# Attention, gated MLP and routed MLP on one Trainium2 core: the attention's value matmuls per head and per half of the array's columns, with two batches side by side

## The chip, the cores and the metric

The kernel runs on one NeuronCore of a Trainium2 chip. The metric is the device time of one execution in microseconds (us), lower is better. The core has TensorE (PE in the profile; PEld is its weight loading), VectorE (DVE), ScalarE (ACT), GpSimd (POOL) and SyncE (SP, which only issues DMAs here). Before the change three runs took 828.89, 834.08 and 834.34 us; the median is 834.08.

## What is computed

Three stages follow each other. Causal attention with a window of 64 keys, 4 batches, 8 heads, 576 tokens, head size 64:

```python
scores = scale * np.matmul(q, k.transpose(0, 1, 3, 2))
mask = (rel >= 0) & (rel < window)
scores = np.where(mask, scores, -1000000000.0)
scores = scores - np.max(scores, axis=-1, keepdims=True)
attn = np.exp(scores)
attn = attn / (np.sum(attn, axis=-1, keepdims=True) + 1e-09)
out = np.matmul(attn, v)
```

Its output becomes x, 2304 tokens by 512. A gated MLP follows (RMS norm, two 512 by 1536 matrices, silu(g) * val, a 1536 by 512 matrix), then a mixture of 8 experts in which each token goes to the one expert with the largest logit (512 to 1024, relu, 1024 to 512, times the gate). All of it is fp32; the MLPs split each operand into two fp32r parts and use three matmuls for one.

## The kernel before, in words

The order of instructions on every engine is written out by hand; nothing is moved by a scheduler. The attention works on units u = 0 to 15, one unit for a batch and a pair of heads (`b, hp = divmod(u, NHP)`), and on groups g = 0 to 47, three groups for a unit, three blocks of 64 queries for a group. The main loop `for g in range(NG + LX)` runs one step for each group and, in the same step, later stages of earlier groups. In step g these are:

- `scores(g)`, TensorE: one bf16 matmul puts the mask into bank g % 3 (384 columns), three fp32 matmuls add the scores of a block each. The stationary operand is `q_t`, 64 queries of head 0 beside 64 queries of head 1 with zeros off the diagonal, so that a block is 128 rows (two heads by 64 queries) by a window of 128 keys.
- `maxima(g)` on VectorE and `softmax(g - 1)` (three Exp) on ScalarE.
- `transposes(g - 3)` on TensorE into bank 3 or 4, and `pt_copy(g - 3)`, which copies 128 by 384 to SBUF, on ScalarE.
- `pv(g - 4)`, line 242, on TensorE: three fp32 matmuls of 128 by 130 columns, 128 values of both heads and two columns of ones for the sum. Only the two diagonal quarters of the result are used. The banks are 5, 6 and 7 in turn.
- `xo_out(g - 5)`, line 250, on VectorE: add 1e-9 to the sums, reciprocal, multiply into an SBUF tile; after a unit's third group two DMAs write it to `xdram` in DRAM, 64 floats at a time.

`q_place(u)` (line 193) fills `qz`, three buffers in turn, from the loaded q, for u from 2 on with two GpSimd instructions of 64 partitions each. It stands two units ahead of the scores that read it. `q_load`, `k_load` and `v_load` issue the loads on SP's queue, in the order of the program.

Beside the steps, `attending_work(g)` (line 524) advances generators a piece at a time: the RMS norms of the first two stretches of 384 tokens (`norm`, line 327, from steps 20 and 31 on, `G_NORM`), which read x back from `xdram`, the splitting of the first weights, and the unpacking of MLP weights on VectorE and ScalarE (`w_conv`), under a budget of `CREDIT` for each step. In the last five steps (48 to 52) the MLP's first matmuls (`first_gv`) are mixed in. After the loop the MLP goes over the 2304 tokens in blocks; `norm(2)` to `norm(5)` run beside it. All matmuls go through one helper on line 60.

Of the kernel before, what the change touches and what calls it, by code (L numbers as in the profile page):

```python
# [8 lines left out]
F32 = mybir.dt.float32  # L9
# [4 lines left out]
ALU = mybir.AluOpType  # L14
# [27 lines left out]

LT, LV, LX = 3, 4, 5
NQK = 3
VW = P + 2
G_MORE = 27, 42
G_LOAD, G_LAND, G_NORM = (3, 8, 13), 5, (15 + LX, 26 + LX)
CREDIT = 0.45
MID = 2.0
BUDGET = [4.6, 3.4, 4.7, 5.4]  # L50
# [3 lines left out]
def attention_moe_moe_kernel(ctx, tc, qT, kT, vw, w1p, rms_g, wg2, wg2T, w2p, out):  # L54
# [44 lines left out]
        nc.gpsimd.iota(tot, pattern=[[NT // P, E]], base=0, channel_multiplier=0,  # L99
                       allow_small_or_imprecise_dtypes=True)  # L100

    xdram = [dram.tile([S, DM], F32, name=f"xdram{b}") for b in range(B)]
    x2dram = dram.tile([NT + 1, DM], F32, name="x2dram")

    xs = dram.tile([E * NT, DM], F32, name="xs")
# [42 lines left out]
    def place(k, key, what):  # L148
# [3 lines left out]
        if not here:  # L152
# [11 lines left out]
    qz = [f_p.tile([P, NBLK, P], F32, name=f"qz{i}") for i in range(NQK)]  # L164
    vbuf = [t[:, a:a + 8 * VW].rearrange("p (w c) -> p w c", c=VW)
            for t, a in ((wraw_t[3], 0), (wraw_t[3], 8 * VW), (wraw_t[1], 5 * 3 * P))]

    def zeros(i):
        for h in range(2):
# [8 lines left out]
    NG = NU * 3  # L178
    q_t, qs_t, k_t, v_t, xo_t, p_t, pt_t, nm_t = {}, {}, {}, {}, {}, {}, {}, {}

    def q_load(u):
        if u < NU:
            qs_t[u] = a_q.tile([P, 64, NBLK], F32, name="qs")
            nc.sync.dma_start(qs_t[u], qT[u // NHP, u % NHP])

    def k_load(u):
        if u < NU:
            k_t[u] = a_q.tile([P, S], F32, name="kt")
            cuts = [0, 192, S] if u == 0 else [0, S]
            for c in (slice(*x) for x in zip(cuts, cuts[1:])):  # L190
                nc.sync.dma_start(k_t[u][:, c], kT[u // NHP, u % NHP, :, c])

    def q_place(u):
        if u < NU:
# [10 lines left out]
    def v_load(u):  # L205
        if u < NU:
            v_t[u] = vbuf[u % 3]
            nc.sync.dma_start(v_t[u][:, :, :P], vw[u // NHP, u % NHP])

    def scores(g):  # L210
        u, i0 = g // 3, 3 * (g % 3)
# [25 lines left out]

    def pt_copy(g):
        pt = pt_t[g] = wraw_t[1][:, (g % 5) * 3 * P:(g % 5 + 1) * 3 * P]
        nc.scalar.copy(pt, bank[3 + g % 2][:, 0:3 * P])  # L240

    def pv(g):
        u, i0 = g // 3, 3 * (g % 3)
        pt = pt_t.pop(g)
        for j in range(3):
            i = i0 + j
            w = 0 if i <= 1 else (i // 2 if i % 2 else 3 + i // 2)
            mm(bank[5 + g % 3][:, j * VW:(j + 1) * VW], pt[:, j * P:(j + 1) * P], v_t[u][:, w], True, True)

    def xo_out(g):  # L250
        u, i0 = g // 3, 3 * (g % 3)
        b, hp = divmod(u, NHP)
        if g % 3 == 0:
            t, a = ((wraw_t[4], 3 * DM), (wraw_t[5], 3 * DM), (wraw_t[2], 5 * 3 * P))[u % 3]
            xo_t[u] = t[:, a:a + 2 * S].rearrange("p (i c) -> p i c", c=P)
        vb = bank[5 + g % 3][:, 0:3 * VW].rearrange("p (j c) -> p j c", j=3)
        rs = a_s.tile([P, 3], F32, name="rs")
        nc.vector.tensor_scalar(out=rs, in0=vb[:, :, P], scalar1=1e-9, scalar2=None, op0=ALU.add)
        nc.vector.reciprocal(rs, rs)
        nc.vector.tensor_tensor(out=xo_t[u][:, i0:i0 + 3], in0=vb[:, :, :P], in1=rs.unsqueeze(2).to_broadcast([P, 3, P]),  # L260
                                op=ALU.mult)
        if g % 3 == 2:
            for h in range(2):
                r = slice(64 * h, 64 * h + 64)
                nc.sync.dma_start(xdram[b].rearrange("(i q) (a d) -> a q i d", q=64, d=64)[2 * hp + h], xo_t[u][r, :, r])

    class Task:

# [58 lines left out]
    def norm(i):  # L327
        t0, nt, _ = subs[i]
        T = nt // P
        if i == 1:  # L330

            xr, sq = (t[:, :3 * DM].rearrange("p (j d) -> p j d", d=DM) for t in wraw_t[:-3:-1])
        else:
            if i > 2:
                yield "step"
            xr, sq = big(0), big(1)
        for j in range(T):
            p = 0
            while p < P:
                b, s = divmod(t0 + j * P + p, S)  # L340
                step = min(P - p, S - s)
                nc.sync.dma_start(xr[p:p + step, j], xdram[b][s:s + step])
                p += step
        for _ in range(4 if i < 2 else 1):
            yield "wait" if i < 2 else "step"
        ss, y, t = (n_p.tile([P, 3], F32, name=x)[:, :T] for x in ("ss", "y", "nt"))
        for j in range(T):
            yield "act" if i < 2 else "rest"
            nc.scalar.activation(sq[:, j], xr[:, j], AF.Square, scale=1.0, accum_out=ss[:, j:j + 1])
        yield "wait" if i < 2 else "step"  # L350
        nc.vector.tensor_scalar(out=ss, in0=ss, scalar1=1.0 / DM, scalar2=1e-6, op0=ALU.mult, op1=ALU.add)
        nc.vector.tensor_scalar(out=y.bitcast(I32), in0=ss.bitcast(I32), scalar1=-0.5, scalar2=1597463007.0,
                                op0=ALU.mult, op1=ALU.add)
        sc = 1.0
        for _ in range(NEWTON):

            yield 0.35
            nc.vector.scalar_tensor_tensor(out=t, in0=y, scalar=1.0 / (sc * sc), in1=y, op0=ALU.mult, op1=ALU.mult)
            nc.vector.tensor_mul(t, t, ss)
            nc.vector.scalar_tensor_tensor(out=y, in0=t, scalar=-3.0, in1=y, op0=ALU.add, op1=ALU.mult)  # L360
            sc = sc * -2.0
        yield "wait" if i < 2 else 0.5
        for j in range(T):
            (nc.gpsimd if i < 2 else nc.vector).tensor_scalar(
                out=xr[:, j], in0=xr[:, j], scalar1=y[:, j:j + 1], scalar2=None, op0=ALU.mult)
            yield "wait" if i < 2 else 0.6
        staged[0] = True
        for _ in (4, 2, 0)[min(i, 2)] * [0]:
            yield "wait"
        if i >= NXT:  # L370
            yield lambda: free[0] >= i - NXT + 1
        xh_t[i], xl_t[i] = xh, xl = xt_views(i % NXT * 8 * SUB, nt)
        for c in range(4):
            bk = yield "bank"
            for j in range(T):
                nc.tensor.transpose(bk[:, j * P:(j + 1) * P], xr[:, j, c * P:(c + 1) * P], ident)
            nc.scalar.activation(xh[:, c], bk[:, :nt], AF.Copy, scale=gs_sb[:, c:c + 1])
            if i < 2:
                yield "wait"
            nc.vector.scalar_tensor_tensor(out=xl[:, c], in0=bk[:, :nt], scalar=gs_sb[:, c:c + 1],  # L380
                                           in1=xh[:, c].bitcast(F32), op0=ALU.mult, op1=ALU.subtract)
            if c < 3 and i > 1:
                yield 0.6
        normed[0] = i
        yield 0.6
# [138 lines left out]
    def attending_work(g):  # L524
        if not w64:
            ready.update(range(4))
        for i in st_t:
            loaded.setdefault(i, g)
        landed.update(i for i in st_t if g >= loaded[i] + G_LAND)
        tasks = [norm0] * (g >= G_NORM[0]) + [norm1] * (g >= G_NORM[1]) + [early] * (g >= G_LOAD[0])  # L530
        late[0] = g >= NG - 10
        for _ in range(2 if ending[0] else 1):
            busy = False
            for t in tasks + [acts] * w64:
                if not t.done and (t.want in (None, "wait") or t.want == "act" and not busy):
                    if t.want == "act":
                        busy = True
                    t.piece()
        c = min(credit[0] + (1.0 if ending[0] else CREDIT), 1.0 if ending[0] else 0.6)
        tasks = [t for t in tasks + [conv] if not t.done and t.want not in ("wait", "act")]  # L540
        if any(t.want == "bank" for t in tasks):
            on_bank(tasks, bank[5 + (g - 2) % 3])
            c -= 0.6
        if g >= G_LOAD[0] and converted[0] < 2:
            c = beside(tasks, c)
        elif g >= G_LOAD[0]:
            c = beside(tasks[:-1], c)
        credit[0] = c
# [31 lines left out]
    for g in range(NG + LX):  # L580
        if g == NG:
            ending[0] = True
            convert(1, conv)
            early.finish()
            norm0.finish(bank[2])
        if g < NG:
            if g % 3 == 0:
                q_load(g // 3 + 3)
# [3 lines left out]
            scores(g)  # L592
        if 0 <= g - LT < NG:
            transposes(g - LT)
        if 0 <= g - LV < NG:
            pv(g - LV)
        if g >= NG:
            for _ in range(2):
                next(first_gv, None)
        if 0 <= g - LT < NG:  # L600
            pt_copy(g - LT)
        if 0 <= g - LX < NG:
            xo_out(g - LX)
        if g < NG:
            maxima(g)
        if 0 < g <= NG:
            softmax(g - 1)
        if 0 < g < NG and g % 3 == 0:
# [6 lines left out]
        if g == 0:  # L615
            zeros(2)
            for v in vbuf:
                nc.vector.memset(v[:, :, P:], 1.0)
            q_place(2)
            constants()  # L620
        if g == 1:
# [657 lines left out]
```

## Time and profile before

| | us |
|---|---|
| three runs, median | 834.08 (828.89 to 834.34) |
| the profiled execution, its own time | 828.35 |
| its span, first to last instruction | 826.6 |
| attention, first score matmul to the first matmul of the MLP's second layer | 4.3 to 111.2 |

The profiled execution is 5.73 us below the median and close to the fastest run. The profile counts a matmul as busy until its result is out, so the starts of successive matmuls, not their durations, tell what one costs; every fp32 matmul stands as two matmul records (and two weight loads), so three matmuls of the program are six in a row. "x6" behind a row is the number of instructions merged in it. The idle time at a row's end is that of the engine just before, with what ended it.

### The profile page before, as it was taken

Reading aid. Unit: us, or ns where it says so; the run is one execution under the profiler, and the core shown is the slowest. Engines: PE = TensorE matmul, PEld = TensorE weight load, DVE = VectorE, ACT = ScalarE, POOL = GpSimd, SP = SyncE. Lnnn points to the kernel's source line nnn. Section 1 sums busy time; section 2 is a strip of 40 time slices with the busy share of each in tenths; the row PEclk is TensorE's granted clock in tenths of the full one; section 3 lists DMA queues with packets and bytes.
Section 4 is the critical chain, followed back from the end, with each engine's and each line's share of the span. In section 5 each row is a group of like instructions: output and inputs, shape, how many; then the busy total and the mean of one; then the engine's idle time right before and its main releaser. Section 6 shows DMA issues by size and latency. Waiting matters only on the chain. (4 is left out here: it accounts for less than half of the span.)

```text
span 826.6 us, 13258 instructions
## 1 busy us (share of the span) xinstructions
PE 806.6 (98%) x4777; PEld 746.5 (90%) x4777; DVE 566.7 (69%) x1210; ACT 431.1 (52%) x839; POOL 222.1 (27%) x194
## 2 busy tenths in 40 slices
PE   7999999999999999999999999999899999999997
PEld 7999989899999999999899999999788999888886
DVE  6898777777754766763389869846595765776454
ACT  5878877677633323322343333434564654765353
POOL 7989444334340000015000006031300220222021
PEclk9999999999999999999999999999999999999999
DMA  8999679889422101002110023861675763772010
GB/s 273 327 294 303 154 183 249 224 174 273 128 103 77 38 1 39 1 1 76 40 38 1 1 81 112 266 170 62 159 252 193 232 231 113 260 252 81 2 45 22
DMA packets 76179, 114.33 MB, mean 138 GB/s; under 512 B 28847, under 2 KB 45615, under 8 KB 75954
## 3 DMA queue, kind: packets, MB, share of 16 engines
q1 hardware_dynamic: 71506, 103.50, 42.5%
q0 software_dynamic: 4576, 9.47, 3.1%
q8 instruction: 69, 1.13, 0.6%
q14 instruction: 28, 0.23, 0.1%
HBM read 93.90 MB, written 31.10 MB: 151 GB/s over the span
## 5 line engine op out<-in xcount | busy, mean ns | idle before, releaser
L60 PE MATMUL bank<-xt,wha 128*128 128x384 f32 (+3 forms) x1728 | 417.9, 327 | 1.9 <-ACT xt L892 1.3
L60 PEld LDWEIGHTS bank<-xt,wha 128*128 128x128 f32 x1728 | 301.8, 188 | 10.9 <-ACT xt L892 1.5
L60 PE MATMUL bank<-xt,wla 128*128 128x384 f32 (+3 forms) x864 | 280.0, 324 | 0.3 <-DVE wla L576 0.3
L60 PEld LDWEIGHTS bank<-xt,wla 128*128 128x128 f32 x864 | 162.7, 188 | 1.0 <-DVE wla L576 0.6
L60 PE MATMUL bank<-who,hl 128*128 128x512 f32 x382 | 150.2, 393 | 1.0 <-DVE hl L1058 0.6
L60 PE MATMUL bank<-who,hh 128*128 128x512 f32 x382 | 150.3, 393 | 0.2 <-ACT x L1086 0.2
L60 PE MATMUL bank<-wlo,hh 128*128 128x512 f32 x382 | 149.4, 391 | 0.0
L685 ACT CAST hh<-t 128x384 fp32r<-128x384 f32 x72 | 37.0, 514 | 149.4 <-DVE t L684 149.4
L576 DVE TENSOR_TENSOR wla<-wraw,wha 128x512 fp32r<-128x512 f32 (+1 forms) x113 | 99.2, 878 | 15.9 <-ACT wha L574 15.2
L1058 DVE SCALAR_TENSOR_TENSOR hl<-bank,hh 128x512 fp32r<-128x512 f32 (+1 forms) x71 | 44.7, 629 | 70.9 <-ACT hh L1057 70.8
L684 DVE TENSOR_TENSOR t<-t,bank 128x384 f32<-128x384 f32 x72 | 39.7, 552 | 74.1 <-PE bank L60 67.9
L574 ACT CAST wha<-wraw 128x512 fp32r<-128x512 f32 (+1 forms) x113 | 87.0, 770 | 6.0 <-DVE wraw L426 5.8
L1087 POOL DMA_INDIRECT out_dram<-x,ix x32 | 34.8, 1086 | 204.1 <-ACT x L1086 196.6
L60 PEld LDWEIGHTS bank<-who,hl 128*128 128x128 f32 x382 | 71.8, 188 | 18.2 <-DVE hl L1058 1.4
L1057 ACT ACTIVATE hh<-bank 128x512 fp32r<-128x512 f32 (+1 forms) x71 | 39.0, 550 | 89.3 <-PE bank L60 89.3
L60 PEld LDWEIGHTS bank<-who,hh 128*128 128x128 f32 x382 | 72.0, 189 | 10.4 <-ACT x L1086 0.4
L60 PEld LDWEIGHTS bank<-wlo,hh 128*128 128x128 f32 x382 | 72.0, 189 | 10.2
L574 ACT CAST who<-wraw 128x512 fp32r<-128x512 f32 x111 | 68.7, 619 | 17.5 <-PE bank L60 17.5
L749 DVE SCALAR_TENSOR_TENSOR junk<-x,wg_bc 128x512 f32<-128x512 f32 x120 | 76.6, 685 | 0.0
L576 DVE TENSOR_TENSOR wlo<-wraw,who 128x512 fp32r<-128x512 f32 x99 | 68.2, 689 | 8.6 <-ACT who L574 3.4
L683 ACT ACTIVATE t<-bank 128x384 f32<-128x384 f32 x72 | 35.0, 486 | 65.7 <-PE bank L60 62.7
L797 POOL TENSOR_TENSOR tot<-tot,ohb 128x8 f32<-128x8 f32 x18 | 4.5, 251 | 237.6 <-DVE de L781 236.5
(154 smaller groups left out, 969.9 us busy)
## 6 DMA issues: line engine op xcount, KB each, us to landing
wraw<-in_w2p_dram SPq DMA_DIRECT2D x64, 512.0 KB, 4.6
st<-in_w1p_dram SPq DMA_DIRECT2D x24, 768.0 KB, 7.3
wraw<-in_vw_dram SPq DMA_DIRECT2D x16, 512.0 KB, 5.9
xs<-x2dram SPq DMA_DIRECT2D x8, 1024.0 KB, 12.8
qs<-in_qT_dram SPq DMA_DIRECT2D x16, 288.0 KB, 5.9
xdram<-wraw SPq DMA_DIRECT2D x32, 144.0 KB, 4.6
x2dram<-x SPq DMA_DIRECT2D x18, 256.0 KB, 2.0
kt<-in_kT_dram SPq DMA_DIRECT2D x15, 288.0 KB, 5.4
```

Of the source, the lines that this page charges most:

```text
L60: nc.tensor.matmul(o, l, r, start=start, stop=stop)
L574: nc.scalar.copy(wh, src[:, r])
L576: e.tensor_tensor(out=wl, in0=src[:, r], in1=wh.bitcast(F32), op=ALU.subtract)))
L683: nc.scalar.activation(t, g, AF.Silu, scale=1.0)
L684: nc.vector.tensor_tensor(out=t, in0=t, in1=v, op=ALU.mult)
L685: nc.scalar.copy(hh[:, :nt], t)
L749: nc.vector.scalar_tensor_tensor(out=junk, in0=x2, scalar=1.0, in1=wg_bc[:, e], op0=ALU.mult, op1=ALU.mult, accum_out=lg[:, j, e:e + 1])
L797: nc.gpsimd.tensor_tensor(out=tot, in0=tot, in1=ohb[:, j], op=ALU.add)
L1057: nc.scalar.activation(hh[:, :n], bank[k % 2][:, :n], AF.Relu, scale=1.0)
L1058: nc.vector.scalar_tensor_tensor(out=hl[:, :n], in0=bank[k % 2][:, :n], scalar=0.0, in1=hh[:, :n].bitcast(F32), op0=ALU.max, op1=ALU.subtract)
L1087: d = nc.gpsimd.indirect_dma_start(out=out[:, :], in_=y, in_offset=None, out_offset=bass.IndirectOffsetOnAxis(ap=ix[:, j, 0:1], axis=0), b ...
```

## The change

`of(u)` lets units of two batches alternate: units 0, 2, 4, 6 are batch 0 and 1, 3, 5, 7 batch 1, for the four pairs of heads; units 8 to 15 are batches 2 and 3. Two successive units make a super-unit of 18 blocks, of which two successive blocks are 128 tokens. `pv(d)` now takes six blocks, once in two steps. For each pair of blocks, head and block of the pair it issues one matmul with 64 stationary columns (the head's 64 queries) and 66 moving columns (the head's 64 values and two ones); the block decides whether the result goes to partitions 0 to 63 or 64 to 127. Twelve such matmuls fill one bank (6 or 7) as 128 tokens by two heads, three times. `xo_out(d)` divides this once in two steps. For the first two batches it writes straight into `x_sb`, three SBUF tiles in places of `wraw` that are free then, which `norm(0)` to `norm(2)` read without a DMA. For the other two it writes to `xdram`, 128 floats at a time. `pt_copy` of even groups moves from ScalarE to VectorE, behind `maxima`. Bank 5 is now free for the norms' transposes. The norms start at steps 25 and 33, and two weight loads move (`G_MORE`).

```diff
-VW = P + 2
-G_MORE = 27, 42
-G_LOAD, G_LAND, G_NORM = (3, 8, 13), 5, (15 + LX, 26 + LX)
+VW = P + 4
+G_MORE = 21, 44
+G_LOAD, G_LAND, G_NORM = (3, 8, 13), 5, (20 + LX, 28 + LX)
...
+    x_sb = [wraw_t[t][:, a:a + 3 * DM].rearrange("p (j d) -> p j d", d=DM) for t, a in ((4, 0), (4, 3 * DM), (5, 0))]
...
+    def of(u):
+        return 2 * (u // (2 * NHP)) + u % 2, u % (2 * NHP) // 2
...
     def pt_copy(g):
         pt = pt_t[g] = wraw_t[1][:, (g % 5) * 3 * P:(g % 5 + 1) * 3 * P]
-        nc.scalar.copy(pt, bank[3 + g % 2][:, 0:3 * P])
-
-    def pv(g):
-        u, i0 = g // 3, 3 * (g % 3)
-        pt = pt_t.pop(g)
+        (nc.scalar.copy if g % 2 else nc.vector.tensor_copy)(pt, bank[3 + g % 2][:, 0:3 * P])
+
+    def pv(d):
+        su, n0 = d // 3, 6 * (d % 3)
         for j in range(3):
-            i = i0 + j
-            w = 0 if i <= 1 else (i // 2 if i % 2 else 3 + i // 2)
-            mm(bank[5 + g % 3][:, j * VW:(j + 1) * VW], pt[:, j * P:(j + 1) * P], v_t[u][:, w], True, True)
+            for h in range(2):
+                for c in range(2):
+                    n = n0 + 2 * j + c
+                    u, i, at = 2 * su + n // NBLK, n % NBLK, n % 3 * P + 64 * h
+                    w = 0 if i <= 1 else (i // 2 if i % 2 else 3 + i // 2)
+                    mm(bank[6 + d % 2][64 * c:64 * c + 64, j * VW + 66 * h:j * VW + 66 * h + 66],
+                       pt_t[6 * su + n // 3][:, at:at + 64], v_t[u][:, w, 66 * h:66 * h + 66], True, True)
...
-        nc.vector.tensor_scalar(out=rs, in0=vb[:, :, P], scalar1=1e-9, scalar2=None, op0=ALU.add)
+        nc.vector.tensor_scalar(out=rs, in0=vb[:, :, 0:VW:VW - 2], scalar1=1e-9, scalar2=None, op0=ALU.add)
         nc.vector.reciprocal(rs, rs)
-        nc.vector.tensor_tensor(out=xo_t[u][:, i0:i0 + 3], in0=vb[:, :, :P], in1=rs.unsqueeze(2).to_broadcast([P, 3, P]),
-                                op=ALU.mult)
-        if g % 3 == 2:
-            for h in range(2):
-                r = slice(64 * h, 64 * h + 64)
-                nc.sync.dma_start(xdram[b].rearrange("(i q) (a d) -> a q i d", q=64, d=64)[2 * hp + h], xo_t[u][r, :, r])
+        nc.vector.tensor_tensor(out=xo.rearrange("p j (h d) -> p j h d", h=2),
+                                in0=vb[:, :, 2:P + 2].rearrange("p j (h d) -> p j h d", h=2),
+                                in1=rs.unsqueeze(3).to_broadcast([P, 3, 2, 64]), op=ALU.mult)
+        if bp:
+            rows = slice(part * 3 * P, (part + 1) * 3 * P)
+            nc.sync.dma_start(xdram[rows, cols].rearrange("(j p) c -> p j c", p=P), xo)
...
-            on_bank(tasks, bank[5 + (g - 2) % 3])
+            on_bank(tasks, bank[6 + (g - 3) // 2 % 2] if g % 2 else bank[5])
...
-        if 0 <= g - LV < NG:
-            pv(g - LV)
+        if 0 <= g - LV < NG and (g - LV) % 2:
+            pv((g - LV) // 2)
```

On TensorE, two steps in the middle of the attention, before. The rows are line, operation, output bank, moving and stationary operand; bank 65 to 67 hold scores, 68 and 69 transposes, 70 to 72 values:

```order
L60 LDWEIGHTS ident_b
L60 MATMUL bank_67<-maskb,ident_b 128x384
L60 MATMUL bank_67<-kt,qz_159 128x128 x3
L236 MATMUL bank_69<-ident,wraw_123 128x128 x3
L60 MATMUL bank_71<-wraw_122 128x130 x3
L60 LDWEIGHTS ident_b
L60 MATMUL bank_65<-maskb,ident_b 128x384
L60 MATMUL bank_65<-kt,qz_160 128x128 x3
L236 MATMUL bank_68<-ident,wraw_123 128x128 x3
L60 MATMUL bank_72<-wraw_122 128x130 x3
```

The same place now:

```order
L60 LDWEIGHTS ident_b
L60 MATMUL bank_67<-maskb,ident_b 128x384
L60 MATMUL bank_67<-kt,qz_156 128x128 x3
L240 MATMUL bank_69<-ident,wraw_120 128x128 x3
L60 LDWEIGHTS ident_b
L60 MATMUL bank_65<-maskb,ident_b 128x384
L60 MATMUL bank_65<-kt,qz_157 128x128 x3
L240 MATMUL bank_68<-ident,wraw_120 128x128 x3
L60 MATMUL bank_71<-wraw_119 64x66 x12
```

The three value matmuls of each step became twelve in every second step, each a quarter of the size, with the full array in use right before and right behind them.

On VectorE, two steps of the same stretch, before (the sums, reciprocal, product and maxima of a step):

```order
L258 TENSOR_SCALAR rs<-bank_71 128x3
L259 RECIPROCAL rs<-rs 128x3
L260 TENSOR_TENSOR wraw_125<-bank_71,rs 128x384
L224 TENSOR_REDUCE nm<-bank_65 128x3
L258 TENSOR_SCALAR rs<-bank_72 128x3
L259 RECIPROCAL rs<-rs 128x3
L260 TENSOR_TENSOR wraw_125<-bank_72,rs 128x384
L224 TENSOR_REDUCE nm<-bank_66 128x3
```

Two steps now:

```order
L268 TENSOR_SCALAR rs<-bank_72 128x6
L269 RECIPROCAL rs<-rs 128x6
L270 TENSOR_TENSOR wraw_123<-bank_72,rs 128x3x128
L228 TENSOR_REDUCE nm<-bank_66 128x3
L228 TENSOR_REDUCE nm<-bank_67 128x3
L244 COPY wraw_119<-bank_68 128x384
```

One division for two steps instead of two, and a copy that ScalarE did.

## Rows read from the trace of the kernel before

**Rows 1.** The page: span, TensorE's busy time, granted clock in 40 slices.
```profile
span 826.6 us, 13258 instructions
PE 806.6 (98%) x4777; PEld 746.5 (90%) x4777; DVE 566.7 (69%) x1210; ACT 431.1 (52%) x839; POOL 222.1 (27%) x194
...
PEclk9999999999999999999999999999999999999999
```

**Rows 2.** Busy by window: PE, PEld, DVE, ACT, POOL; clock, DMA share, GB/s.
```profile
12.50:93.00 80.50, 79.12 (x687) 77.47 (x685) 70.55 (x202) 65.92 (x197) 71.30 (x41) 1.00 1.04 305
93.00:108.00 15.00, 12.69 (x93) 11.75 (x91) 9.59 (x27) 9.30 (x23) 2.62 (x3) 1.00 0.25 44
```

**Rows 3.** Timeline of PE: one step at 59 us, and the start of step 45.
```profile
59.05 0.33 PE L60 MATMUL bank<-maskb,ident_b 128*128 128x384 bf16 x1
59.21 0.83 PE L60 MATMUL bank<-kt,qz 128*128 128x128 f32 x6
59.88 0.49 PE L236 MATMUL bank<-ident,wraw 128*128 128x128 f32 x3
60.20 0.83 PE L60 MATMUL bank<-wraw 128*128 128x130 f32 x6
60.88 0.33 PE L60 MATMUL bank<-maskb,ident_b 128*128 128x384 bf16 x1
...
89.33 0.33 PE L60 MATMUL bank<-maskb,ident_b 128*128 128x384 bf16 x1
```

**Rows 4.** Groups by form, 0 to 110 us: count, busy, mean ns, idle before.
```profile
L60 PE MATMUL bank<-wraw,wraw 128*128 128x130 f32 x198 | 27.6, 276 | 0.1
...
L260 DVE TENSOR_TENSOR wraw<-bank,rs 128x384 f32<-128x384 f32 x48 | 26.8, 558 | 1.6
L224 DVE TENSOR_REDUCE nm<-bank 128x3 f32<-128x384 f32 x48 | 26.4, 550 | 2.6 <-PE bank L60 1.4 <-PE bank L236 0.4 <-issue 0.3
L259 DVE RECIPROCAL rs<-rs 128x3 f32<-128x3 f32 x48 | 8.4, 176 | 1.7
L258 DVE TENSOR_SCALAR rs<-bank 128x3 f32<-128x3 f32 x48 | 7.4, 154 | 4.8 <-PE bank L60 4.7
...
L240 ACT COPY wraw<-bank 128x384 f32<-128x384 f32 x48 | 25.1, 523 | 12.9 <-PE bank L236 12.7
...
L202 POOL TENSOR_SCALAR qz<-qs 64x576 f32<-64x576 f32 x29 | 65.1, 2244 | 9.4 <-DMA qs<-in_qT_dram 6.6 <-PE bank L236 0.7 <-PE bank L376 0.4
```

**Rows 5.** Timeline of PE: small bf16 and fp32 matmuls of the routing.
```profile
368.25 0.27 PE L60 MATMUL bank<-ohb,ones_b 128*128 128x40 bf16 x5
368.37 0.18 PE L60 MATMUL bank<-totb,ones_b 128*128 128x48 bf16 x1
...
539.72 0.18 PE L60 MATMUL bank<-short,ones_b 1*128 1x24 bf16 x1
539.83 0.19 PE L60 MATMUL bank<-totb,ones_b 128*128 128x24 bf16 x1
...
566.22 2.74 PE L60 MATMUL bank<-wg_sb,x 128*128 128x8 f32 x24
568.81 0.37 PE L60 MATMUL bank<-xt,wha 128*128 128x256 f32 x1
```

**Rows 6.** Timeline of POOL in the attention.
```profile
16.12 32.91 POOL L202 TENSOR_SCALAR qz<-qs 64x576 f32<-64x576 f32 x14
...
66.14 4.67 POOL L364 TENSOR_SCALAR xr<-xr,y 128x512 f32<-128x512 f32 x3
...
80.32 4.50 POOL L202 TENSOR_SCALAR qz<-qs 64x576 f32<-64x576 f32 x2 [0.16 <-DMA qs<-in_qT_dram]
84.91 1.29 POOL L518 TENSOR_TENSOR wla<-wraw,wha 128x512 fp32r<-128x512 f32 x1
```

**Rows 7.** DMA queue and issues, 12.5 to 93 us: packets, MB, share; count, KB.
```profile
q1 hardware_dynamic: 35794, 24.38, 103.2%
...
xdram<-wraw SPq DMA_DIRECT2D x26, 144.0 KB, 4.9
```

**Rows 8.** Waits, 0 to 110 us: in total, times, longest.
```profile
PE bank L376 <- DVE wraw L260: 2.0, 2, 1.0
```

More of the change, by code (lines that the diff above doesn't have):

```diff
@@ L100, in constants @@
                        allow_small_or_imprecise_dtypes=True)
-    xdram = [dram.tile([S, DM], F32, name=f"xdram{b}") for b in range(B)]
+    xdram = dram.tile([NT // 2, DM], F32, name="xdram")
     x2dram = dram.tile([NT + 1, DM], F32, name="x2dram")
@@ L183, in q_load @@
             qs_t[u] = a_q.tile([P, 64, NBLK], F32, name="qs")
-            nc.sync.dma_start(qs_t[u], qT[u // NHP, u % NHP])
+            nc.sync.dma_start(qs_t[u], qT[of(u)])
     def k_load(u):
@@ L190, in k_load @@
             for c in (slice(*x) for x in zip(cuts, cuts[1:])):
-                nc.sync.dma_start(k_t[u][:, c], kT[u // NHP, u % NHP, :, c])
+                nc.sync.dma_start(k_t[u][:, c], kT[of(u)][:, c])
     def q_place(u):
@@ L207, in v_load @@
             v_t[u] = vbuf[u % 3]
-            nc.sync.dma_start(v_t[u][:, :, :P], vw[u // NHP, u % NHP])
+            nc.sync.dma_start(v_t[u][:, :, 2:P + 2], vw[of(u)])
     def scores(g):
@@ L250, in xo_out @@
[L250 to L257, printed above, removed]
-        nc.vector.tensor_scalar(out=rs, in0=vb[:, :, P], scalar1=1e-9, scalar2=None, op0=ALU.add)
-        nc.vector.reciprocal(rs, rs)
-        nc.vector.tensor_tensor(out=xo_t[u][:, i0:i0 + 3], in0=vb[:, :, :P], in1=rs.unsqueeze(2).to_broadcast([P, 3, P]),
-                                op=ALU.mult)
-        if g % 3 == 2:
-            for h in range(2):
-                r = slice(64 * h, 64 * h + 64)
-                nc.sync.dma_start(xdram[b].rearrange("(i q) (a d) -> a q i d", q=64, d=64)[2 * hp + h], xo_t[u][r, :, r])
+            for h in range(2):
[5 more added lines that the diff above has]
+                       pt_t[6 * su + n // 3][:, at:at + 64], v_t[u][:, w, 66 * h:66 * h + 66], True, True)
@@ new lines, in xo_out @@
+    def xo_out(d):
+        su, part = divmod(d, 3)
+        bp, hp = divmod(su, NHP)
+        cols = slice(hp * P, (hp + 1) * P)
+        if bp == 0:
+            xo = x_sb[part][:, :, cols]
+        else:
+            t, a = ((wraw_t[5], 3 * DM), (wraw_t[2], 5 * 3 * P))[hp % 2]
+            xo = t[:, a + part * 3 * P:a + (part + 1) * 3 * P].rearrange("p (j c) -> p j c", c=P)
+        vb = bank[6 + d % 2][:, 0:3 * VW].rearrange("p (j c) -> p j c", j=3)
+        rs = a_s.tile([P, 3, 2], F32, name="rs")
+        nc.vector.tensor_scalar(out=rs, in0=vb[:, :, 0:VW:VW - 2], scalar1=1e-9, scalar2=None, op0=ALU.add)
+        nc.vector.reciprocal(rs, rs)
+        nc.vector.tensor_tensor(out=xo.rearrange("p j (h d) -> p j h d", h=2),
[4 more added lines that the diff above has]
+            nc.sync.dma_start(xdram[rows, cols].rearrange("(j p) c -> p j c", p=P), xo)
@@ L329, in norm @@
         T = nt // P
-        if i == 1:
-            xr, sq = (t[:, :3 * DM].rearrange("p (j d) -> p j d", d=DM) for t in wraw_t[:-3:-1])
-        else:
-            if i > 2:
-                yield "step"
+        if i < 3:
+            xr, sq = x_sb[i], big(1 - i % 2)
+        else:
+            yield "step"
             xr, sq = big(0), big(1)
[L337 to L345, printed above, removed]
+            rows = slice(t0 - NT // 2, t0 - NT // 2 + nt)
+            nc.sync.dma_start(xr[:, :T], xdram[rows].rearrange("(j p) d -> p j d", p=P))
+            yield "step"
         ss, y, t = (n_p.tile([P, 3], F32, name=x)[:, :T] for x in ("ss", "y", "nt"))
@@ L584, in attention_moe_moe_kernel @@
             early.finish()
-            norm0.finish(bank[2])
+            norm0.finish(bank[5])
         if g < NG:
@@ L599, in attention_moe_moe_kernel @@
                 next(first_gv, None)
-        if 0 <= g - LT < NG:
+        if 0 <= g - LT < NG and (g - LT) % 2:
             pt_copy(g - LT)
-        if 0 <= g - LX < NG:
-            xo_out(g - LX)
+        if 0 <= g - LX < NG and (g - LX) % 2:
+            xo_out((g - LX) // 2)
         if g < NG:
             maxima(g)
+        if 0 <= g - LT < NG and (g - LT) % 2 == 0:
+            pt_copy(g - LT)
         if 0 < g <= NG:
@@ L617, in attention_moe_moe_kernel @@
             for v in vbuf:
-                nc.vector.memset(v[:, :, P:], 1.0)
+                nc.vector.memset(v[:, :, 0:2], 1.0)
+                nc.vector.memset(v[:, :, P + 2:], 1.0)
             q_place(2)
```

## The prediction

> **What bounds the kernel now.** I read the page first. TensorE is busy for 806.6 of 826.6 us at the full clock in every slice [rows 1], so the end moves only if TensorE has less to do, waits less, or waits more. The change touches the attention alone, so the windows come next: from 12.5 to 93 us TensorE is busy for 79.12 of 80.5 us, but VectorE (70.55), GpSimd (71.30) and the DMA engines (share 1.04) stand close behind it [rows 2]. From 93 to 108 us, where the attention ends and the MLP begins, TensorE idles more, 12.69 of 15.00 busy [rows 2].
>
> Busy time counts a matmul until it is out, so a step is read from starts. A step takes 60.88 - 59.05 = 1.83 us: mask 0.16, scores 0.67, transposes 0.32, values 0.68 [rows 3]. The next step's mask follows the values without a gap, so in this stretch the step is nothing but TensorE's issue time. All 48 steps hold such a value group: 6 records at 0.113 us. What counts is thus the time of two value groups, 1.35 us, against that of one new group of twelve matmuls (24 records).
>
> **Value matmuls: the new group.** A record now moves 66 columns instead of 130 and loads 64 stationary columns instead of 128. If both scale, a record takes half of 0.113, say 0.056 us. Successive pairs of records go to different halves of the columns. No row of before has a matmul in half the columns, so the bounds are far apart:
>
> - The two halves run side by side: 12 times 0.056 = 0.67 us.
> - They run one after the other: 24 times 0.056 = 1.34 us.
> - A record gets no shorter with half the columns: the 24 matmuls of only 8 moving columns still follow each other at (568.81 - 566.22)/24 = 0.108 us [rows 5], since each needs 128 columns of fp32 weights first. Then 24 times 0.108 = 2.59 us.
>
> The nearest rows speak for a shorter record. The bf16 matmuls behind one another, with 128 stationary columns each, come every (368.37 - 368.25)/5 = 0.024 us [rows 5]; so the array can take more weight columns in a given time than one fp32 load uses, and the issue of a record costs no more than 0.024. I take 0.67 us, with 0.67 and 2.59 as ends.
>
> The Trainium skill, "TensorEngine Tiling (Array Packing)", section Key Properties, says that tiles are independent and that different ones can load and multiply in parallel; by it the sum is the 0.67 that I take, and no row here shows it. Another page, "TensorE: Matmul & The Clock Gate", Part 3, The mechanism, has a rule against the change: a load overlaps running matmuls only where it goes to other row groups, and the halves share all rows. By that rule the group would take 2.6 us, the third case above. For the full array the trace disagrees: 128-column loads lie beside matmuls of the same rows, or the records of rows 3 could not follow at 0.11 us.
>
> **Switching between the two uses of the array.** Each new group has a switch ahead and one behind. The nearest row is a matmul with one stationary row between full ones: the next starts 539.83 - 539.72 = 0.11 us after it, where 0.024 is usual [rows 5], so 0.09 more. Behind fp32 work the pipeline is longer: three transposes take 0.49 us with starts 0.11 apart, so one is 0.27 long and a full drain costs 0.27 - 0.11 = 0.16. Ends 0 and 0.16; I take 0.12, or 0.24 for a group. The new group costs 0.67 + 0.24 = 0.91 us against 1.35: 0.44 saved in two steps.
>
> **What the faster step runs into.** GpSimd's q placement is next. It works without a pause from 16.12 to 49.03 us, 14 instructions [rows 6], two for a unit, at 4.7 us for a unit; three old steps are 5.49, three new ones 4.83. Two early groups (steps 5 and 7) gain nothing, since the scores of units 2 and 3 wait for GpSimd. Later GpSimd still has 12 instructions of 2.244 [rows 4] = 26.9, the first norm's three (4.67) and one weight split (1.29) [rows 6] before unit 15 is placed: 49.03 + 32.9 = 81.9 us at the earliest. Step 45, which needs unit 15, starts at 89.33 [rows 3]. So up to there at most 7.4 us can go, where 19 groups at 0.44 would give 8.4. GpSimd also waits for its q loads in places (6.6 us of idle time, start included, in rows 4); I take off 1.0 and count 6.4. Three groups come after step 45: 1.3.
>
> **VectorE and ScalarE.** In two steps VectorE loses one division, 0.558 + 0.176 + 0.154 = 0.89 us, and gains a copy of 128 by 384, not in the trace on this engine; ScalarE's takes 0.523 and VectorE's maxima of the same shape 0.550 [rows 4]. I take 0.53, so 0.36 less in two steps and 24 times 0.36 = 8.6 in all; ScalarE loses 12.5. The window shrinks about as much, so VectorE stays near 88% busy. Value nothing. What stands behind the copy on VectorE is the division or the maxima of the next step; the copy waits only for transposes that are half a step old, and its reader comes more than a step later.
>
> **DMAs.** 26 writes of 144 KB in runs of 256 bytes [rows 7] become, for the first half of the attention, none, and for the second 12 of 192 KB in runs of 512; the reads of three norms go too. They stand on SP's queue ahead of q, k and v loads and wait there for VectorE. TensorE does not wait for them now, so value nothing; but the q loads come more freely, which is why I do not take more than 1.0 off above. If they didn't, GpSimd would be the later one.
>
> **The end of the attention.** The norm's transposes twice wait 1.0 us for a value bank that VectorE has not emptied [rows 8]. Bank 5 is now free for every second of them. Ends 0 and 2.0; I take 1.0. The norms start later by five and two steps but lose the four steps in which they waited for their loads; they still end in the same steps, so nothing. The MLP's instructions behind that stand in the same order, and TensorE is the bound there, so what is saved arrives at the end.
>
> **Sum.** 6.4 + 1.3 + 1.0 = 8.7 us off the profiled execution of 828.35, or 819.7. That execution was 5.73 below the median of the runs, so for a median I take 8.7 off 834.08: 825.4 us. Its own range, with switches of 0 to 0.16 and the tail, is 821 to 831.
>
> **Rivals.**
>
> - *One after the other.* If the halves share something, the group takes 1.34 + 0.24 = 1.58 us, 0.23 more than now, 24 times, less 1.0 at the tail: 4.5 us slower, 838.6. For it: no row shows two matmuls at once. Against it: rows 5, in which the weight path takes far more than one fp32 load.
> - *A record is not shorter,* because with half the columns a weight load no longer lies under the matmul ahead. The place is every second step's value group, the price 2.59 + 0.24 - 1.35 = 1.48 us, 24 times, less 1.0: 34.5 slower, 868.6. It decides from 0.046 us a record on, (1.35 - 0.24)/24, where the group costs what two old ones did. For it: the 0.108 of the 8-column matmuls; against it: loads lie under matmuls everywhere in the full array.
> - *Another engine takes the gain.* VectorE at 88%, with unpacking and norm pieces in bursts, and DMA engines at a share of 1.03 [rows 7] allow a step of 1.83 but perhaps not one of 1.6. Then some 3 us are left: 831. For it: four resources within 12% of each other [rows 2]; against it: VectorE, ScalarE and the DMAs all get less work in two steps, about as much less as TensorE.
>
> **How the numbers follow.** Forecast 0.52, other engine 0.10, one after the other 0.20, no shorter record 0.18. A change of 1% (8.3 us) is about what a measurement of this kernel can tell from none. Faster by more: 0.42, most of the forecast's share, since 8.7 is barely beyond that. Within 1%: 0.10 of the forecast, 0.10 for the other engine, 0.16 of one after the other, 0.36. Slower: 0.04 + 0.18 = 0.22. The range reaches down to 817, since runs scatter by 5 us, and up to 842 past the second case, which leaves the third out.
>
> **What would show it.** Right: two successive steps in 3.22 us instead of 3.66, the twelve matmuls over in about 0.9 us from the last transpose to the next mask, starts of the two halves nearly together, VectorE's copy near 0.53, GpSimd's q placement without long pauses, and step 45 some 6 us sooner. Wrong: 24 starts evenly 0.056 or 0.11 apart, a gap over 0.2 us at the switches, or TensorE waiting in mid attention for `qz`, for VectorE's copy or for a value bank.

## The result and the profile after

The changed kernel takes 819.04 us (median of four runs, 817.68 to 821.07) beside 832.10 of the kernel before (four runs, 828.89 to 834.34): 0.9848 of it, with a 95% interval of 0.9803 to 0.9893. Measured again on two other occasions the ratio is 0.9832 (0.9798 to 0.9866), 817.6 us beside 830.73, and, with two runs alone (814.28 and 815.20), 0.9815 (0.974 to 0.989) beside 830.53. It is faster by over 1%, as forecast; the forecast of 825.4 us is 6.4 too high, and inside its range the time lies near the low end.

The page of the changed kernel, first execution profiled (821.07 us), beside [rows 1]:

```profile
span 819.3 us, 13641 instructions
PE 797.6 (97%) x5065; PEld 732.0 (89%) x5065; DVE 557.8 (68%) x1165; ACT 421.3 (51%) x815; POOL 221.4 (27%) x194
...
PEclk9999999999999999999999999999999999999999
```

TensorE has 9 us less to do, although its matmul records rose from 4777 to 5065: each old value matmul became two of a quarter of its size. The windows beside [rows 2], cut at step 47 as there (columns PE, PEld, DVE, ACT, POOL, clock, DMA share, GB/s):

```profile
12.50:87.00 74.50, 71.11 (x938) 64.66 (x936) 63.14 (x158) 58.28 (x177) 72.07 (x42) 1.00 0.88 270
87.00:102.00 15.00, 14.75 (x148) 13.46 (x147) 11.69 (x25) 9.32 (x22) 5.09 (x4) 1.00 0.54 155
```

The first window is 6 us shorter at the same clock. TensorE waits 3.4 us in it, where it waited 1.4 before; GpSimd is busy for 97% of it instead of 89, VectorE for 85 instead of 88. In the second TensorE is busy for 14.75 of 15 us instead of 12.69.

Two steps on TensorE, to be read against [rows 3], and the start of step 45:

```profile
61.48 0.92 PE L60 MATMUL bank<-wraw,wraw 128*64 128x66 f32 x24
62.33 0.34 PE L60 MATMUL bank<-maskb,ident_b 128*128 128x384 bf16 x1
...
64.75 0.92 PE L60 MATMUL bank<-wraw,wraw 128*64 128x66 f32 x24
65.61 0.34 PE L60 MATMUL bank<-maskb,ident_b 128*128 128x384 bf16 x1
...
82.93 0.33 PE L60 MATMUL bank<-maskb,ident_b 128*128 128x384 bf16 x1
```

From mask to mask, two steps take 65.61 - 62.33 = 3.28 us instead of 3.66. The 24 records of a value group stand in one row, 0.92 long. How they follow each other shows at 58 us, where the two halves read their values from differently named buffers and are not merged into one row:

```profile
58.09 0.22 PE L60 MATMUL bank<-wraw 128*64 128x66 f32 x1
58.10 0.22 PE L60 MATMUL bank<-wraw,wraw 128*64 128x66 f32 x1
58.15 0.22 PE L60 MATMUL bank<-wraw 128*64 128x66 f32 x1
58.16 0.22 PE L60 MATMUL bank<-wraw,wraw 128*64 128x66 f32 x1
58.22 0.22 PE L60 MATMUL bank<-wraw 128*64 128x66 f32 x1
58.22 0.45 PE L60 MATMUL bank<-wraw,wraw 128*64 128x66 f32 x9
58.61 0.34 PE L60 MATMUL bank<-maskb,ident_b 128*128 128x384 bf16 x1
```

Records start in pairs, one for each half of the columns, 0.01 apart, and the pairs come every 0.06 us. So the halves do run side by side, and a record with half the columns costs half. The groups by form, beside [rows 4] (count, busy, mean ns, idle before):

```profile
L270 DVE TENSOR_TENSOR wraw<-bank,rs 128x384 f32<-128x384 f32 x24 | 13.4, 558 | 0.8
L244 DVE COPY wraw<-bank 128x384 f32<-128x384 f32 x24 | 13.1, 548 | 0.0
```

The division stands 24 times instead of 48 at the same 558 ns, and VectorE's copy takes 548. GpSimd, beside [rows 6], and the DMAs, beside [rows 7]:

```profile
15.97 46.23 POOL L206 TENSOR_SCALAR qz<-qs 64x576 f32<-64x576 f32 x20
62.30 3.13 POOL L366 TENSOR_SCALAR wraw<-wraw,y 128x512 f32<-128x512 f32 x2
...
70.00 1.59 POOL L366 TENSOR_SCALAR wraw<-wraw,y 128x512 f32<-128x512 f32 x1
...
77.40 4.55 POOL L206 TENSOR_SCALAR qz<-qs 64x576 f32<-64x576 f32 x2
```

```profile
q1 hardware_dynamic: 22775, 19.94, 86.8%
...
xdram<-wraw SPq DMA_DIRECT2D x8, 192.0 KB
```

GpSimd works from 15.97 to 81.95 us without a pause worth naming, on q and, in between, on the first norm's scaling and one weight split. The DMA queue's share is 86.8% instead of 103.2. TensorE's waits, 0 to 101 us, beside [rows 8] (total, times, longest):

```profile
PE bank L60 <- DVE qz L206: 4.4, 1, 4.4
PE bank L60 <- POOL qz L206: 1.7, 2, 1.0
PE bank L378 <- POOL wraw L366: 1.2, 1, 1.2
```

The 4.4 us for VectorE is the start of the program. The two waits for a value bank are gone; in their place stand three for GpSimd, 2.9 us in all, where there was one of 0.6. The first two are for q of units 2 and 3:

```profile
15.05 0.94 PE L60 MATMUL bank<-kt,qz 128*128 128x128 f32 x6 [0.98 <-POOL qz L206]
...
20.52 0.94 PE L60 MATMUL bank<-kt,qz 128*128 128x128 f32 x6 [0.77 <-POOL qz L206]
```

The third, at 71.65 us, is for the first norm's scaling. From unit 4 on every placement is done at least 0.8 us before its scores start, that of unit 15 1.1 us before (81.95 and 83.09).

Where the time went, from the starts of TensorE's rows. Both kernels were profiled again beside the experiments, so before has two executions and the changed kernel three:

| stretch, us | before | changed |
|---|---|---|
| start of step 45 | 89.33, 89.24 | 82.93, 83.46, 83.15 |
| from there to the first matmul of the MLP's second layer | 21.83, 21.80 | 18.20, 18.22, 18.20 |
| from there 36 matmuls of that form (`who`, `hh`) on | 78.35, 77.98 | 77.57, 77.55, 77.55 |
| the next 180 of them | 375.23, 375.21 | 375.21, 375.21, 375.22 |
| the rest, to the end of the span | 261.9, 261.9 | 265.4, 259.0, 261.8 |

The attention gives 9.7 us, the first block of the MLP 0.6, together 10.3. The rest scatters by 6 us between executions of one kernel and gains nothing on average; in the first execution of the changed kernel 3.2 us of it are waits for nothing that the profile shows, which were 0 and 0.6 in the other two. The medians of the timed runs differ by 13; both profiled executions of before (828.35 and 827.88) lie below the median of its runs (829.6 to 830.7 in later comparisons), so what makes its median run 2 to 3 us longer is in no trace here.

### The profile page after: what moved, and what is told of

It reads as the page before. It is cut to its first block, busy times and chain, and to the rows that moved or that the text cites. A ratio compares the mean times of both kernels' runs of the same rounds, so it can differ in the third digit from the quotient of the medians.

```text
span 819.3 us, 13641 instructions
## 1 busy us (share of the span) xinstructions
PE 797.6 (97%) x5065; PEld 732.0 (89%) x5065; DVE 557.8 (68%) x1165; ACT 421.3 (51%) x815; POOL 221.4 (27%) x194
## 4 chain that ended last, share of the span: by engine, by line
PE 82%; issue 6%; DVE 4%; POOL 3%; ACT 2%; DMA 2%; SPq 0%; POOLq 0%; ACTq 0%; DVEq 0%
PE bank L60 79%; POOL qz L206 2%; PE bank L895 1%; PE bank L240 1%; PE bank L378 1%; DMA sq<-xs 1%; DMA qs<-in_qT_dram 1%; POOL wraw L366 1%; DVE wla L578 1%; POOL out_dram L1092 1%; DVE wlo L578 1%; DVE xt L898 0%; DVE wraw L428 0%; ACT gt L465 0%; ACT wha L576 0%
## 5 line engine op out<-in xcount | busy, mean ns | idle before, releaser
L60 PEld LDWEIGHTS bank<-who,hh 128*128 128x128 f32 x382 | 71.9, 188 | 10.3 <-ACT x L1091 0.4
```

The costliest lines, as they stand in the source:

```text
L60: nc.tensor.matmul(o, l, r, start=start, stop=stop)
```

## The experiments

Since the rest scatters, each kernel is compared by its time and by the end of its attention, the start of the MLP's first second-layer matmul: 111.1 us before, 101.1 to 101.7 for the changed kernel.

**All of one half, then all of the other.** The same twelve matmuls, in an order that gives no neighbours in different halves.

```diff
-        for j in range(3):
-            for h in range(2):
-                for c in range(2):
+        for j, h, c in [(j, h, c) for c in range(2) for j in range(3) for h in range(2)]:
```

> The changed kernel with one edit: in a value group all twelve records of the first half of the columns come first, then all twelve of the second, so that only one pair can lie side by side. Same number and size of matmuls, same layouts, DMAs and copies. Theory (the gain is that the two halves run side by side): the group takes 23 times 0.058 = 1.33 us instead of 12 times 0.058 = 0.70, 0.63 more in two steps, 24 times 15 us; about 4 us of it hides in the waits for GpSimd's q placement that the changed kernel has, so 830 us (826 to 834), close to the kernel before. Rival (the gain comes from x staying in SBUF, from fewer small DMAs or from the moved copy): 819, unchanged.

Measured: 826.09 us, 0.9951 of before (0.9931 to 0.9972), at the low end of the theory's range. A value group in its timeline:

```profile
59.86 1.44 PE L60 MATMUL bank<-wraw 128*64 128x66 f32 x24
61.23 0.34 PE L60 MATMUL bank<-maskb,ident_b 128*128 128x384 bf16 x1
```

From the first record to the next mask the group takes 61.23 - 59.86 = 1.37 us instead of 62.33 - 61.48 = 0.85. The attention ends at 110.6, hardly earlier than before the change. So running side by side is worth 9 us of the attention's 9.7, and without it the change is worth about 4 us (0.5% of the time), of which 2.1 lie in the part that scatters (259.8 us here, 261.9 before).

**Two neighbours in one half, two in the other.** The loops over head and half change places.

```diff
-            for h in range(2):
-                for c in range(2):
+            for c in range(2):
+                for h in range(2):
```

> The changed kernel with two loops of a value group exchanged (the half outside, the head inside): four records go to one half, then four to the other. Theory: only the records at a change of half lie side by side, 5 of 24, so 19 times 0.058 = 1.10 us instead of 0.70, 0.40 more in two steps, 9.6 us in 24 groups, of which some 3 hide in the waits for GpSimd: 825 us (822 to 829), between the changed kernel and the one with all of a half first. Rival: 819.

Measured: 817.30 us, 0.9847 (0.9825 to 0.9869): no slower than the changed kernel, and the expectation missed. Its timeline, by the two names of the halves' operands:

```profile
58.55 0.51 PE L60 MATMUL bank<-wraw 128*64 128x66 f32 x9
58.85 0.26 PE L60 MATMUL bank<-wraw,wraw 128*64 128x66 f32 x1
...
58.95 0.22 PE L60 MATMUL bank<-wraw,wraw 128*64 128x66 f32 x1
58.96 0.22 PE L60 MATMUL bank<-wraw 128*64 128x66 f32 x1
...
59.46 0.34 PE L60 MATMUL bank<-maskb,ident_b 128*128 128x384 bf16 x1
```

The group takes 59.46 - 58.55 = 0.91 us, 0.06 more than in the changed kernel; 24 times that is 1.4, and its attention ends at 102.8, 1.4 later. Records of the two halves start side by side (58.95 and 58.96) although four records in a row are for one half. So the pairing is not one of neighbours: each half takes its next record when it is free, some records ahead of the program's order. In the run before, by the starts of the single records, the second half's first one is at 60.386, ahead of the last three of the first half (60.438, 60.495, 60.553). No earlier one overlaps, and in all 24 groups the second half starts just behind the ninth of the first half's twelve records, so the look-ahead ends after a few records. The 0.06 us of this run fit that: once in a group the load of the second half's fifth record starts only behind the first half's fifth record (58.844 and 58.840), not behind its own fourth (58.797), and the record after it comes 0.10 later instead of 0.06. In both runs a load that waits for the second copy of the transposes stands close by; in the changed kernel the same load is not late (61.714, behind a record at 61.712), so this wait alone does not explain it, but what sets the limit is not shown.

**Two more switches for each group.** The first four matmuls of a group stand ahead of the step's transposes, the other eight behind.

```diff
-        for j in range(3):
+        for j in js:
...
+        if 0 <= g - LV < NG and (g - LV) % 2:
+            pv((g - LV) // 2, (0,))
```

> The changed kernel with the value group cut in two: the first four of its twelve matmuls stand ahead of the step's transposes, the other eight behind them, so that TensorE switches four times in two steps between the full array and halves, not twice. Same matmuls. Theory (a switch costs about 0.09 us, as the starts around the group in the changed kernel's trace show): 0.2 us more in two steps, 24 times 4.6, of which 1 to 2 hide in waits for GpSimd: 821 to 823 against 818 to 819 for the changed kernel. Rival 1 (a switch costs nothing, the gap belongs to the matmuls): no change. Rival 2 (a switch costs the whole drain of 0.16 or more and delays the transposes): 825 or more.

Measured: 821.74 us, 0.9902 (0.9871 to 0.9933), inside the theory's 821 to 823. The split group:

```profile
59.22 0.34 PE L60 MATMUL bank<-maskb,ident_b 128*128 128x384 bf16 x1
...
61.31 0.46 PE L60 MATMUL bank<-wraw 128*64 128x66 f32 x8
61.70 0.55 PE L240 MATMUL bank<-ident,wraw 128*128 128x128 f32 x3
62.18 0.27 PE L60 MATMUL bank<-wraw 128*64 128x66 f32 x1
62.19 0.27 PE L60 MATMUL bank<-wraw,wraw 128*64 128x66 f32 x1
62.29 0.22 PE L60 MATMUL bank<-wraw 128*64 128x66 f32 x1
...
62.80 0.34 PE L60 MATMUL bank<-maskb,ident_b 128*128 128x384 bf16 x1
```

Two steps take 62.80 - 59.22 = 3.58 us, 0.30 more than 3.28, for two switches more: 0.15 each. The theory had 0.2 for both. The row at 62.18 shows a part of it: the first pair holds its place for 0.11 us (to 62.29), where later pairs take 0.06. By the starts of the single records 0.09 more go ahead of that pair and 0.09 behind the last, and the first transpose behind a group holds its place 0.06 longer than the others. The attention ends at 107.4, 6 us later; 24 times 0.30 would be 7.2.

**The copy back on ScalarE.**

```diff
-        (nc.scalar.copy if g % 2 else nc.vector.tensor_copy)(pt, bank[3 + g % 2][:, 0:3 * P])
+        nc.scalar.copy(pt, bank[3 + g % 2][:, 0:3 * P])
```

> The changed kernel with the copy of the transposes of even groups back on ScalarE. Theory: neither engine sets the step, so 819 (817 to 821). Rival (ScalarE was close to the bound, and the moved copy is part of the gain): ScalarE gets 0.5 us more in two steps, up to 6 us slower, 822 to 825.

Measured: 821.42 us, 0.9893 (0.9871 to 0.9916), between the two; the attention ends at 103.6, 2.2 later. Its window:

```profile
12.50:88.00 75.50, 71.90 (x935) 64.21 (x934) 55.49 (x139) 64.65 (x195) 71.78 (x41) 1.00 0.86 267
```

VectorE is busy for 55.49 us and ScalarE for 64.65, where the changed kernel has about 64 and 59; TensorE waits for ScalarE's Exp four times, 1.5 us in all, instead of once or twice and 0.3 to 0.8. With all the copies ScalarE is busy for 86% of the shorter stretch, and TensorE now waits for it at times. The move does not bring the gain, but it lets some 2 us of it through.

**x of the first two batches through DRAM.** All super-units write to DRAM, and `norm(0)` to `norm(2)` read back, the first two with four steps of waiting as before.

```diff
-        if bp == 0:
-            xo = x_sb[part][:, :, cols]
-        else:
...
-        if bp:
...
+            nc.sync.dma_start(xr[:, :T], xdram[t0:t0 + nt].rearrange("(j p) d -> p j d", p=P))
+            for _ in range(4 if i < 2 else 1):
+                yield "wait" if i < 2 else "step"
```

> The changed kernel, but x of the first two batches goes to DRAM and back as that of the other two: 12 more writes of 192 KB in runs of 512 bytes, and norms 0 to 2 load 768 KB each (and wait four steps for it, as before the change). Value matmuls and the copy as in the changed kernel. Theory: TensorE doesn't wait for these DMAs, so 819 to 821. Rival (x staying in SBUF brings a good part of the 13 us): 825 or more.

Measured: 827.59 us, 0.9973 (0.9957 to 0.9989): the theory's number missed by 7, and the time is the rival's. TensorE's waits, 8 to 115 us:

```profile
PE bank L60 <- DMA wraw<-in_vw_dram: 3.7, 1, 3.7
PE bank L377 <- DVE t L688: 3.6, 1, 3.6
PE bank L377 <- POOL short L901: 1.1, 1, 1.1
```

One value group stands 3.7 us for its v load, which on SP's queue is behind the norm's read, and that waits for the writes of x; at the end the norm is late, 4.7 us. The attention ends at 113.3, 11.9 later than in the changed kernel. These waits are 8.4 of it. Behind each of the two long ones TensorE's granted clock stands at the lower of its two levels (1.2 of 2.4 GHz): 0.50 from 63.2 to 66.6 us and 0.51 from 107.5 to 111.0, about 1.7 us of lost work each (an estimate: half of the stretch). With pairs of batches the first 384 tokens are complete only at step 24, where one batch alone had them at step 16, so there is no time left for the way through DRAM. x in SBUF is not a gain against the kernel before, which did not wait for that way; it is what the new order needs.

**Some of GpSimd's q on ScalarE.** The second head's placement for units 3, 13, 14 and 15 goes to ScalarE.

```diff
-                    if h == 1 and u < 2:
+                    if h == 1 and u in (0, 1, 3, 13, 14, 15):
```

> The changed kernel, but the second half of q's placement for units 3, 13, 14 and 15 is done by ScalarE (1.2 us each) instead of GpSimd (2.25 us each). Theory (after the change GpSimd's q placement is the bound around step 9 and from step 39 on, where the trace shows TensorE waiting for it): 2 to 4 us faster than the changed kernel, 815 to 817, and step 45 starts near 79 us instead of 82.9. Rival (another resource is right behind, or ScalarE then delays the Exps): within 1 us of the changed kernel, 818 to 820.

Measured: 817.94 us, 0.9846 (0.9799 to 0.9892), the rival's (the two runs of the changed kernel beside it took 814.28 and 815.20); the attention ends at 102.5. Its window and waits (12.5 to 88 and 8 to 112 us):

```profile
12.50:88.00 75.50, 71.02 (x931) 64.26 (x930) 63.78 (x157) 63.07 (x181) 62.91 (x37) 1.00 0.86 265
```

```profile
PE bank L60 <- DVE xt L382: 1.7, 2, 1.2
PE bank L60 <- ACT wraw L235: 1.3, 3, 0.7
```

GpSimd falls from 73 to 62.91 us busy, and TensorE waits for VectorE and ScalarE (3.0 us) instead. The expectation took its waits from the wrong units: of the four units moved, TensorE had waited for the placement of unit 3 alone (0.77 us); units 13 to 15 were placed 1.1 us or more ahead of their scores. This does not tell whether GpSimd bounds the step, since ScalarE got what GpSimd lost.

**GpSimd's work left out.** Seven of its placements are skipped, and nothing is put on another engine.

```diff
+                    if h == 1 and u in (3, 5, 7, 9, 11, 13, 15):
+                        continue
```

> Leaves out the placement of the second head's q for units 3, 5, 7, 9, 11, 13 and 15 (seven GpSimd instructions of 2.24 us, 15.7 us of GpSimd's time, nothing added elsewhere), so that those scores are computed from an older unit's q. Theory (GpSimd's placement caps the gain, as the prediction had it): without it the 19 groups ahead of step 45 give their measured 0.38 us each, 7.2 us, and the wait of 1.2 us for the norm's scaling on GpSimd goes too; step 45 starts at 81 to 82 us instead of 82.9 to 83.5, the chain's share of GpSimd vanishes, and the time is 1 to 2.5 us under the changed kernel's. Rival (VectorE and ScalarE stand equally close, as the run with q on ScalarE suggested): the waits reappear as waits for VectorE or ScalarE in the same places, step 45 stays at 82.9 to 84.4 and the time within 1 us of the changed kernel's.

Measured: 813.63 us, 0.9784 (0.9745 to 0.9824). Step 45:

```profile
81.69 0.33 PE L60 MATMUL bank<-maskb,ident_b 128*128 128x384 bf16 x1
```

81.69 us, 1.2 to 1.8 sooner than in the changed kernel, as the theory expected, and the wait for the norm's scaling is gone. So GpSimd is the engine that TensorE waits for, and the placements left out cost some 1.5 us: the wait of 0.8 for unit 3 and that of 1.2 for the norm are gone, while that for unit 2, whose placement stays, is 1.3 us here. The time fell by 4, more than that: 2 us of it lie in the part that scatters (259.8 us here).

**A version meant to beat both.** The q of units 2 and 3, for which TensorE waits longest, half on ScalarE.

```diff
-                    if h == 1 and u < 2:
+                    if h == 1 and u < 4:
```

> A version meant to beat both: the second head's q of units 2 and 3 is placed by ScalarE (1.25 us each) as that of units 0 and 1 is, and by GpSimd from unit 4 on. In the changed kernel TensorE's two longest waits in the attention (1.3 us at step 6, 1.1 us at step 9) are for the placement of these two units. If they go and nothing takes their place: 1.5 to 2.5 us less than the changed kernel (about 815 to 817.5). Rival: the softmax queued behind them on ScalarE is late by as much, and the time is the changed kernel's within 1 us.

Measured: 820.63 us, 0.9872 (0.9841 to 0.9902): worse than the changed kernel. ScalarE and TensorE at the start:

```profile
10.55 1.22 ACT L204 ACTIVATE qz<-qs 64x576 f32<-64x576 f32 x1 [2.27 <-DMA qs<-in_qT_dram]
11.79 2.44 ACT L235 ACTIVATE wraw<-bank,nm 128x128 f32<-128x128 f32 x9
```

```profile
12.73 0.48 PE L60 MATMUL bank<-maskb,ident_b 128*128 128x384 bf16 x1 [3.59 <-DMA x2dram<-sq]
```

ScalarE stands for 2.27 us until q of unit 2 has landed, and nine Exps of steps before wait behind it; TensorE waits 3.59 us for a bank (the releaser in the row is a DMA long done; the first three Exps, which read the bank, end at about 11.79 + 2.44/3 = 12.6). In the changed kernel it is GpSimd that waits for this load, with no Exps behind it. The pause costs more than its length. TensorE's granted clock behind it, here and in the changed kernel:

```profile
12.70:18.60 5.90, 5.87 (x27) 5.67 (x27) 1.67 (x3) 3.93 (x11) 3.08 (x8) 0.50 0.99 330
```

```profile
12.70:18.60 5.90, 4.92 (x74) 4.19 (x73) 3.71 (x10) 3.22 (x12) 5.63 (x10) 1.00 1.03 332
```

For 5.9 us TensorE, busy throughout, runs at the lower of its two levels, about 3 us of lost work (an estimate: half of the stretch). The waits for q of units 2 and 3 are gone, as meant, yet the attention ends at 105.2, 3.9 later. No version here beats the changed kernel by more than the runs scatter.

**The changed kernel again**, beside the last two:

> The changed kernel itself, beside the two runs before, for a ratio on the same chip: 815 to 820 us, 0.980 to 0.989 of the kernel before.

Measured: 817.6 us (814.82 to 820.59), as said above.

## Why the prediction held, step by step

- *Side by side, 0.67 us.* Held. It was a choice between 0.67 and 2.59 that no row of before could settle, as the prediction says. Pairs come every 0.059 us (by the starts of single records in the group at 61.48: (62.174 - 61.585)/10), 12 times that is 0.71. The rival of one half after the other is the first experiment, and the rival of a record that gets no shorter falls with it: there a record of one half alone takes 0.058. Its rule from the Trainium skill, "TensorE: Matmul & The Clock Gate", Part 3, The mechanism, that a load overlaps only where it goes to other row groups, is not borne out: the halves share all rows, each load's record is 0.14 us long, and at 0.059 us a pair no load lies outside the matmuls.
- *Two switches, 0.12 each.* Held. From the last transpose to the first value record go 0.20 us instead of 0.11, and the first pair takes 0.05 more than the others; behind the last pair the mask starts 0.10 later than a pair would. That is 0.24, and the group comes to 0.95 instead of 0.91. Two steps were forecast at 3.22 us and take 3.28; the extra switches of the experiment cost 0.15 each.
- *GpSimd's cap, 6.4 us until step 45.* The number held, by luck in part; the way it came about did not. The last placement ends at 81.95 us (forecast 81.9), and step 45 starts 5.8 to 6.4 sooner. But it does not wait for that placement: the scores of unit 15 start 1.1 to 1.2 us behind it in all three executions, and the 19 groups gave 0.38 each, 7.2, which is less than the 7.4 that the cap allowed. What brings 7.2 down to about 6 is the wait of 1.2 us for the first norm's scaling on GpSimd, which the prediction counted in GpSimd's work but not as a wait of TensorE. That GpSimd has no time left was right, and so were the waits for units 2 and 3. Leaving placements out gave 7.6.
- *After step 45, 1.3 + 1.0.* Mis-sized: 3.6 us came. The term for the end of the attention was taken as 1.0, between 0 and 2.0. Both waits for a value bank in [rows 8] are gone whole, 2.0 us, and a wait of 0.3 for ScalarE with them; the three groups at 0.38 gave 1.1.
- *VectorE, ScalarE, value nothing.* Right in the sum, and the copy at 0.53 (548 ns) too. But the move is not idle: with the copy on ScalarE 2.2 us of the gain are lost.
- *DMAs, value nothing.* Right against the kernel before; the new order depends on it.
- *The MLP, value nothing.* 0.6 us off, in its first block, where TensorE waits once instead of twice 0.4 us for a norm.
- *The base.* 8.7 us was taken off the median of three runs, 834.08. The same kernel later had medians of 829.64, 830.53 and 830.73 in 17, 17 and 11 runs. So of the 6.4 us that 825.4 is too high, some 3.5 are the base; 1.6 are the sum, 8.7 where the traces show 10.3; the last 1.3 are in no trace. The mechanism's own range, 821 to 831, does not reach down to 819.04; only the allowance for scatter, down to 817, does. Nor does that range follow from its terms: switches of 0 to 0.16 and a tail of 0 to 2.0 give savings of 7.5 to 10.4 us, or 823.7 to 826.6.

Of the rivals, "another engine takes the gain" holds in part: some 1.5 us go to GpSimd, by the placements left out.

## What to carry to other kernels

Where only diagonal quarters of a matmul's result are used, splitting it over the two column halves of the array can halve its time, if a group is long enough for two switches of 0.12 to 0.15 us; collect such matmuls into one group rather than two. Before moving work to an engine with free time, ask what the instruction waits for, and what then stands behind it in that engine's order: a load awaited on ScalarE held up Exps that TensorE needed. A long pause of TensorE can cost more than its length, since here the work behind pauses of 3.6 and 3.7 us ran at the lower clock for a time. When an order is changed so that results are complete later, look for every way through DRAM whose time that was.

## What the runs showed of the hardware

The two column halves of the array behave as two streams that need not start in the program's order: records of one half start up to a few records ahead of earlier ones for the other half (60.386 ahead of 60.438 to 60.553). The Trainium skill, "TensorE: Matmul & The Clock Gate", Part 3, The mechanism, has matmuls start strictly in the program's order; for different column halves these starts disagree with that.

The rest of the program scatters partly by the clock. In the stretch of the routing, in which TensorE runs matmuls of 8 columns and is never idle in the records, the granted clock differs between executions of the same kernel. The changed kernel, first profile and a later one:

```profile
554.00:566.00 12.00, 12.00 (x76) 10.64 (x75) 7.83 (x30) 4.80 (x11) 1.43 (x4) 0.86 0.00 0
```

```profile
554.00:566.00 12.00, 12.00 (x89) 10.68 (x88) 8.76 (x32) 5.69 (x12) 2.24 (x6) 1.00 0.04 16
```

At a mean of 0.86 the matmuls of 256 and 512 columns behind the small ones start at the distance of the lower of the two levels (1.2 GHz) from 558.0 to 561.5 us, at 1.00 at that of 2.4; the first took 1.5 us longer from the same matmul to the same. Six of the 13 profiled executions show it behind these matmuls, both of the kernel before and two of the three of the changed kernel among them, so it is no part of the gain. What decides it is not settled here.
